# Entry of a recurrent attention layer: four layer norms and the masks at its head, V of the last tokens through seven SBUF tiles

## The chip, the cores and the metric

One core of a Trainium2 chip runs the whole program. The metric is the time of one execution on the device in microseconds (us), as the median of several runs.

The engines are PE (matmul, with PEld for its weight loads), DVE, ACT and POOL (elementwise work), and SP, which here only issues DMAs. Each engine works through its own queue in order.

## The reference

Four layers in a row, A B A B, each `x = x + layer(layernorm(x))` on x of 2048 tokens by 640, bf16 in and out.

- Layer A is causal attention of 32 heads of 20 in four segments of 512 tokens, with a compressive memory. Only its end matters here: an output projection by `a_wo` for each 128 tokens, the residual sum, and its stores.
- Layer B is a recurrent attention with 32 heads of 128. The tokens come in 64 segments of 32. Each step puts 8 memory rows ahead of its 32 tokens:

```
h = concat([mem, xs])                     # 8 + 32 rows
q, k, v = h@Wq, h@Wk, h@Wv                # 32 heads of 128
p = softmax(where(mask, q k^T * scale, -1e9))
o = (p v) @ Wo
mem = o[:8];  outs.append(o[8:])
```

So step s+1 needs the memory rows that step s has made: 64 steps in series, twice.

## The kernel before, in words

The functions `layer_A` and `layer_B` are called in turn. The arithmetic of layer B stands in one function: pools and constant tiles, then the **entry**, then a loop over 64 steps.

**A step** takes one block of 32 columns (8 memory rows and the first 24 tokens of a segment, in `HX`) through K, Q and V projections ("thin" matmuls, `thin_mm`, lines `b_Ka`, `b_Qa`, `b_Kb`, `b_Qb`, `b_Va`, `b_Vb`), transposes, scores, softmax, P V and the output projection `b_OPS`. The last 8 tokens of each segment ("tails", in `TX`) don't depend on the memory's recurrence in their projections, so they are done for eight segments at once: `tail_unit` makes K or Q of 8 heads for 64 rows, `vtail_unit` makes V of 512 columns for them. Their results go to DRAM (`QKd`, `VTd`, written by `tail_evac` and `vtail_evac`) and come back by segment (`tails_load`, `vtails_in`). There are 8 such units of each kind for a group of eight segments; a step does one of each for the group after.

**The entry** prepares the first group and the first segment:

1. Load four tiles of 128 tokens (`ln_load`, into the tiles xt, XO, XOd and tl of the pool bx), and `b_wv` in five chunks.
2. Layer norm of tiles 0 and 1 (`ln_norm`: DVE statistics, POOL power, DVE normalization), each followed by `ln_spread`: five PE transposes (`b_lntps`) and two ACT copies into `HX` and `TX`.
3. Eight tails (k = 0 to 7). ACT copies the even ones, DVE the odd ones, into `b_tu` tiles that take turns in the four buffers of the pool `kqp`; each copy is followed by a store to `QKd`. The norms of tiles 2 and 3 are put after tails 1 and 5, their spreads after tails 3 and 7.
4. K and Q projections of segment 0's block (`b_Kp`, `b_Qp`), copied by ACT (K) and DVE (Q) into four `b_kq` tiles, which share the four buffers of `kqp` with the tails. The eight chunks of `b_wo` (640 KB each) are loaded behind this in program order. Then transposes (`b_TP`) and copies into KT and QT.
5. `init_state`: two small sums for `b_sel`, zeros for XO, Px, Pm, QZ and HXz, and the additive masks: DVE fills `b_negs` and `b_maskf`, POOL runs 16 selects on `b_maskf`, DVE casts it to `b_mask12`. The tile `b_negs` lies in the buffer of PTa, `b_maskf` in that of OTsb, both in the pool `b_wk`, near the end of SBUF.
6. Eight V units (`vtail_unit(0, k)`), copied by DVE (even) and ACT (odd) into three tiles in turn (vt, E0, msb), each with two stores of 64 rows to `VTd`. Then two V projections (`b_V`), `vtails_in(0)`, and the first tail and V unit of the next group.

**What sets the order.** Inside layer B, `_OrdNC` (lines 89 to 119) chains the instructions of PE, ACT, DVE and POOL to program order, each engine for itself. SP isn't chained. Layer A chains only PE that way. A scheduler that runs when the program is built merges the queues of layer A's end with layer B's entry, with earlier program text first among what is ready. So the entry's first instructions stand in the same queues as layer A's last ones (`a_YP`, `a_xnew`, `a_xnb`).

The pools of a layer are laid over SBUF in the order in which they are opened, behind the constants and `b_wq`, `b_wk`; layer A's pools are closed before layer B's are opened, so both use the same bytes. A tile of layer B waits for the last reader of what lay there. PSUM tiles of layer B's entry (`ps_tile`) share five buffers.

All calls that record an instruction on an engine in this order show as line L101 in the profile (the helper's line), so instructions are named by their tiles. DMAs carry their own lines: L759 `ln_load`, L849 `tail_evac`, L869 `vtail_evac`, L822 `vtails_in`, L660 `b_wo`, L811 `tails_load`, L337 and L340 layer A's stores of x.

Of the kernel before, what the change touches and what calls it, by code (L numbers as in the profile page):

```python
# [18 lines left out]
F32 = mybir.dt.float32  # L19
BF16 = mybir.dt.bfloat16  # L20
# [648 lines left out]
def layer_B(nc, tc, C, W, x_src, xb_src, x_dst, mem0, B_Wv, B_Wo, nsteps=64, out_bf16=False, tag=""):  # L669
    SCB = 1.0 / math.sqrt(128.0)  # L670
    nc_raw = nc
    nc = _OrdNC(tc, nc_raw, engines=ORDER_ENGINES)
# [3 lines left out]
    VTd = tc.dram_tile([nsteps, 8, 4096], BF16, name=f"b_VTd{tag}")  # L676
    with ExitStack() as ctx:
# [6 lines left out]
        bx = pool("b_x", 1)  # L684
        sml = pool("b_sml", 2)
        kqp = pool("b_kqp", 4)
# [3 lines left out]
        wk = pool("b_wk", 1)  # L690
# [12 lines left out]
        Px = st.tile([128, 12, 32], BF16, name="b_Px")  # L703
        Pm = st.tile([128, 12, 32], BF16, name="b_Pm")
        mask12 = st.tile([128, 12, 40], BF16, name="b_mask12")
        QZ = [st.tile([128, 16, 24], BF16, name=f"b_QZ{i}") for i in range(2)]
# [1 line left out]
        HXz = st.tile([128, NCH, 1, 32], BF16, name="b_HXz")  # L708
        OTdef = [wk.tile([128, 32, 32], BF16, name=f"b_OTdef{i}") for i in range(2)]

        def init_state():
            nc.vector.tensor_tensor(out=selm[:, 0, :], in0=C.identb[:, 24:32], in1=C.identb[:, 88:96], op=ALU.add)
            nc.vector.tensor_tensor(out=selm[:, 1, :], in0=C.identb[:, 56:64], in1=C.identb[:, 120:128], op=ALU.add)
            XO_ = bx.tile([64, 320], F32, name="b_XO", tag="XO")
            nc.vector.memset(XO_[:], 0.0)
            XOd_ = bx.tile([64, 320], F32, name="b_XOd", tag="XOd")
            nc.gpsimd.memset(Px[:], 0.0)
            nc.gpsimd.memset(Pm[:], 0.0)
            for i in range(2):
                nc.gpsimd.memset(QZ[i][:], 0.0)  # L720
            negs = wk.tile([128, 32], F32, name="b_negs", tag="PTa")
            nc.vector.memset(negs[:], -1e9)
            maskf = wk.tile([128, 2, 40], F32, name="b_maskf", tag="OTsb")
            nc.vector.memset(maskf[:], 0.0)

            def above(out, rows, ncol, base, chan, colstep=1):
                nc.gpsimd.affine_select(out=out, in_=negs[rows, 0:ncol], pattern=[[colstep, ncol]], compare_op=ALU.is_gt,
                                        fill=0.0, base=base, channel_multiplier=chan)

            for i in range(4):  # L730
                r8, r16, r32 = (slice(32 * i, 32 * i + w_) for w_ in (8, 16, 32))
                above(maskf[r16, 0, 0:8], r16, 8, 8, -1)
                above(maskf[r8, 0, 0:8], r8, 8, 0, -1)
                above(maskf[r32, 1, 8:32], r32, 24, 0, -1)
                above(maskf[r32, 1, 0:8], r32, 8, 24, -1, 0)
            nc.vector.tensor_copy(mask12[:, 0:4, :], maskf[:, 0, :].unsqueeze(1).to_broadcast([128, 4, 40]))
            nc.vector.tensor_copy(mask12[:, 4:12, :], maskf[:, 1, :].unsqueeze(1).to_broadcast([128, 8, 40]))
            nc.gpsimd.memset(HXz[:], 0.0)
            return XO_, XOd_

        HX, TX, QT, KT, VH = {}, {}, {}, {}, {}
        ln_xt, ln_ready = {}, []
# [19 lines left out]
        def ln_norm(g):  # L762
            xt = ln_xt[g]
            layernorm_tile(nc, sml, C, xt[:], xt[:], "b_ln")
            ln_ready.append(g)

        def ln_spread(g):
            xt = ln_xt.pop(g)
            tps = ps_tile([128, NCH, 4, 32], BF16, "b_lntps")
            for c in range(NCH):  # L770
                nc.tensor.transpose(tps[:, c, :, :].rearrange("p i t -> p (i t)"), xt[:, 128 * c:128 * c + 128], C.identb[:])
            HX[g] = hp.tile([128, NCH, 4, 32], BF16, name="b_HX", tag="HX")
            T, half = divmod(g, 2)
            if half == 0:
                TX[T] = tx.tile([128, NCH, 8, 8], BF16, name="b_TX", tag="TX")
            nc.scalar.copy(HX[g][:, :, :, 8:32], tps[:, :, :, 0:24])
            nc.scalar.copy(TX[T][:, :, 4 * half:4 * half + 4, :], tps[:, :, :, 24:32])
# [73 lines left out]
        def vtail_unit(T, k, c0=0, c1=NCH, ps=None):  # L851
            b4, ch = divmod(k, 2)
            if ps is None:
                ps = ps_tile([128, 256], F32, "b_vtail")
            for c in range(c0, c1):
                for q in range(4):
                    n = 2 * b4 + q // 2
                    nc.tensor.matmul(ps[32 * q:32 * q + 32, :], lhsT=TX[T][:, c, 4 * (q % 2):4 * (q % 2) + 4, :].rearrange("p s t -> p (s t)"),
                                     rhs=W.wv[:, c, 512 * n + 256 * ch:512 * n + 256 * ch + 256],
                                     start=(c == 0), stop=(c == NCH - 1), tile_position=(0, 32 * q), skip_group_check=True)  # L860
            return ps

        def vtail_evac(T, k, ps, eng, home="vt"):
            b4, ch = divmod(k, 2)
            vt = wk.tile([128, 256], BF16, name="b_vt", tag=home)
            evac(eng, vt[:], ps[:])
            for jj in range(2):
                o = 512 * (2 * b4 + jj) + 256 * ch
                nc.sync.dma_start(VTd[8 * T:8 * T + 8, :, o:o + 256].rearrange("s t f -> (s t) f"), vt[64 * jj:64 * jj + 64, :])  # L869

        def wo_half(h, jj2):
            return W.wo[:, h, :].rearrange("p (c j x) -> p j c x", j=2, x=64)[:, jj2]
# [14 lines left out]
        n0 = min(4, NG)  # L887
        for g in range(n0):
            ln_load(g, homes[g])
        load_B_wv(nc, W, B_Wv)  # L890
        for g in range(min(2, n0)):
            ln_norm(g)
            ln_spread(ln_ready.pop(0))
        nc.gpsimd.memset(HX[0][:, :, 0, 0:8], 0.0)
        with nc.allow_non_contiguous_dma(reason="mem0 transpose load (tiny)"):
            for c in range(NCH):
# [1 line left out]
        for k in range(8):  # L898
            tail_unit(0, k, 0, 8, shared=True)
            tail_evac(0, k, "act" if k % 2 == 0 else "dve", (kqp, "kq"))  # L900
            if k % 4 == 1 and 2 + k // 4 < n0:
                ln_norm(2 + k // 4)
            if k % 4 == 3 and 2 + k // 4 < n0:
                ln_spread(ln_ready.pop(0))
        cols = cols_of(0)
        jobs = [(nm, b) for b in range(2) for nm in ("K", "Q")]
# [1 line left out]
        for nm, b in jobs:  # L908
            ps = thin_mm(cols, W.wk if nm == "K" else W.wq, b, f"b_{nm}p")
# [9 lines left out]
        XO, XOd = init_state()  # L919
        tails_copy(0, tails_load(0))  # L920
        Vth = VH[-1] = w2.tile([128, 2, 512], BF16, name="b_Vth", tag="Vth")
        for k in range(8):
            vtail_evac(0, k, vtail_unit(0, k), "dve" if k % 2 == 0 else "act", ("vt", "E0", "msb")[k % 3])
        for b in range(2):
            ps = thin_mm(cols, W.wv, b, "b_V")
            evac("act" if b == 0 else "dve", Vth[:, b, :], ps[:])
# [5 lines left out]

        def x_out(ops_, XO_, store, nm):
            nc.vector.tensor_tensor(out=XO_[:], in0=ops_[0:64, :], in1=XO_[:], op=ALU.add)
            if out_bf16:
                xo = wk.tile([64, 320], BF16, name=f"b_xnb{nm}", tag=f"xnb{nm}")
            else:
                xo = XO_
            nc.vector.tensor_tensor(out=xo[:], in0=ops_[64:128, :], in1=XO_[:], op=ALU.add)
            store(xo)  # L940
# [43 lines left out]
        for s in range(nsteps):  # L984
# [183 lines left out]
            if not last:  # L1168
                dst = cols_of(u + 1)
                msb = wk.tile([128, 320], BF16, name="b_msb", tag="msb")  # L1170
# [3 lines left out]
                for pi, (ca, cb) in enumerate(parts):  # L1174
                    mt = ps_tile([128, cb - ca, 8], F32, f"b_MT{pi}")
                    for c in range(ca, cb):
                        for q in range(4):
                            o = 64 * c + 32 * (q % 2)
# [119 lines left out]
```

## Time and profile before

| what | value |
|---|---|
| median of 3 runs | 2735.45 us (2733.53 to 2737.24) |
| the profiled execution | 2729.23 us |
| its span, first to last instruction | 2727.5 us |
| PE busy | 2570.4 us (94%) |
| DVE, ACT, POOL busy | 1688.7, 1580.8, 719.3 us |
| mean granted PE clock | 0.988 of full speed |
| entry of the first layer B: first b_lntps to the first step's b_Ka | 355.33 to 405.82 us |
| the same of the second layer B | 1714.26 to 1761.82 us |
| first step: b_Ka to the next b_Ka | 14.52 us in each |
| PE busy in 355.30 to 390.30, and its granted clock | 28.88 us, 0.79 |
| PE busy in 390.30 to 405.82, and its granted clock | 11.07 us, 0.78 |
| PE busy in 405.82 to 420.34, and its granted clock | 14.27 us, 1.00 |

How to read it: times in the timeline are counted from the span's start. A line of the timeline gives start, duration, engine, operation, tile written and tiles read, shapes and count; in square brackets stands the idle time of that engine before it, and what ended the wait. Where several matmuls are merged into a line, the duration goes to the end of the last, which overlaps the next line's start; the time from start to start is the one to add. The granted clock is the share of PE's full clock that the chip allowed.

### The profile page before, as it was taken

How to read it: one execution, taken by the hardware profiler on the slowest of the kernel's cores; microseconds unless marked ns; L12 is line 12 of the kernel's file. 1: busy time of each engine (PE TensorE's matmuls, PEld its weight loads, DVE VectorE, ACT ScalarE, POOL GpSimd, SP SyncE). 2: the span in 40 equal slices, each digit the busy share in tenths (PEclk: the TensorE clock that was granted, in tenths of full speed). 3: DMA queues.
4: the chain of work that ended last, by engine and by line, in shares of the span. 5: the costliest groups of instructions: out<-in, count | busy, mean ns of one | idle time of the engine just before them, and what ended most of it. 6: DMA issues, size and time to landing. Idle time of an engine off the chain costs nothing. (4 is left out here: it accounts for less than half of the span.)

```text
span 2727.5 us, 146862 instructions
## 1 busy us (share of the span) xinstructions
PE 2570.4 (94%) x65416; PEld 1691.3 (62%) x65480; DVE 1688.7 (62%) x4553; ACT 1580.8 (58%) x3708; POOL 719.3 (26%) x1645
## 2 busy tenths in 40 slices
PE   5999979999999999999989999799999999999998
PEld 3565556666666666666655565566666666666665
DVE  6999935555555555555589998355555555555554
ACT  4998935555555555554459889355555555555543
POOL 4677631111111111111146776211111111111110
PEclk9999979999999999999989999899999999999999
DMA  6111262221212121211130113611111111121110
GB/s 244 38 48 43 70 200 43 46 44 42 45 42 46 43 46 42 43 39 32 25 118 16 64 51 110 180 42 41 40 41 42 42 41 43 38 43 40 38 26 19
DMA packets 322298, 156.34 MB, mean 57 GB/s; under 512 B 245760, under 2 KB 310400, under 8 KB 318592
## 3 DMA queue, kind: packets, MB, share of 16 engines
q1 hardware_dynamic: 320224, 136.47, 19.7%
q8 instruction: 512, 8.39, 1.3%
q10 hardware_dynamic: 1440, 10.49, 1.1%
q14 instruction: 122, 1.00, 0.1%
HBM read 95.15 MB, written 51.71 MB: 54 GB/s over the span
## 5 line engine op out<-in xcount | busy, mean ns | idle before, releaser
L101 PEld LDWEIGHTS <-b_HX 128*32 128x32 bf16 x15360 | 425.5, 97 | 347.3 <-issue 16.2
L101 POOL TENSOR_TENSOR b_Pm<-b_E,b_rs 128x96 bf16<-128x96 bf16 x128 | 63.3, 494 | 1442.4 <-ACT b_Vth L101 1102.8
L130 DVE TENSOR_REDUCE a_nm<-a_S 128x2 f32<-128x512 f32 (+3 forms) x512 | 394.9, 815 | 44.7 <-PE a_S L101 36.9
L130 ACT ACTIVATE a_PT<-a_T 128x1024 bf16<-128x1024 f32 (+1 forms) x384 | 345.0, 902 | 25.9 <-PE a_T L101 17.8
L101 PE MATMUL b_OPS<-b_wo,b_OTsb 128*32 128x320 bf16 x8192 | 309.9, 302 | 11.1 <-issue 8.7
L101 PEld LDWEIGHTS <-b_OTsb 128*32 128x32 bf16 x8192 | 201.6, 97 | 97.8 <-DVE b_OTsb L101 24.5
L101 DVE CAST b_HX<-b_MT 128x8 bf16<-128x8 f32 x372 | 63.5, 172 | 279.1 <-PE b_MT L101 273.9
L130 POOL TENSOR_SCALAR_AFFINE_SELECT a_PT<-a_PT 128x256 bf16<-128x256 bf16 (+1 forms) x384 | 191.1, 509 | 134.8 <-ACT a_PT L130 133.1
L101 ACT CAST b_msb<-b_OPS 128x64 bf16<-128x64 f32 x378 | 69.4, 256 | 237.3 <-PE b_OPS L101 237.3
L101 ACT CAST b_kq<-b_Kb 128x512 bf16<-128x512 f32 x128 | 74.9, 585 | 201.9 <-PE b_Kb L101 201.9
L101 DVE COPY b_KT<-b_TPak 128x128 bf16<-128x128 bf16 x128 | 28.7, 224 | 227.5 <-PE b_TPak L101 227.5
L101 PE MATMUL b_Va<-b_wv,b_HX 128*32 128x512 bf16 x2520 | 160.6, 380 | 0.0
L101 DVE TENSOR_SCALAR b_kq<-b_Qa 128x512 bf16<-128x512 f32 x128 | 88.5, 691 | 116.1 <-PE b_Qa L101 113.3
L101 PE MATMUL b_Vb<-b_wv,b_HX 128*32 128x512 bf16 x2520 | 159.9, 379 | 0.0
L101 PEld LDWEIGHTS <-b_kq 128*128 128x128 bf16 x2080 | 116.8, 98 | 68.8 <-ACT b_kq L101 55.6
L101 PE MATMUL b_Ka<-b_wk,b_HX 128*32 128x512 bf16 x2520 | 159.1, 379 | 0.1
L101 PE MATMUL b_Qa<-b_wq,b_HX 128*32 128x512 bf16 x2520 | 158.8, 379 | 0.0
L101 PE MATMUL b_Kb<-b_wk,b_HX 128*32 128x512 bf16 x2520 | 158.8, 379 | 0.0
L101 PE MATMUL b_Qb<-b_wq,b_HX 128*32 128x512 bf16 x2520 | 158.7, 379 | 0.0
L101 DVE CAST b_OTsb<-b_OTP 128x160 bf16<-128x160 f32 (+1 forms) x384 | 122.2, 373 | 39.9 <-PE b_OTP L101 39.9
L101 PE MATMUL b_vtail<-b_wv,b_TX 128*32 128x256 bf16 x2880 | 136.9, 271 | 7.8 <-issue 4.7
L101 PE MATMUL a_T<-a_q,a_kT 32*128 32x512 bf16 (+3 forms) x1024 | 121.6, 299 | 23.5 <-DVE a_nm L130 16.1
(194 smaller groups left out, 5723.7 us busy)
## 6 DMA issues: line engine op xcount, KB each, us to landing
b_QKd<-b_tu SPq DMA_DIRECT2D x128, 128.0 KB
b_tl<-b_QKd SPq DMA_DIRECT2D x128, 128.0 KB
b_wv<-in_B_Wv_dram SPq DMA_DIRECT2D x10, 1024.0 KB
b_wo<-in_B_Wo_dram SPq DMA_DIRECT2D x16, 640.0 KB
b_VTd<-b_vt SPq DMA_DIRECT2D x256, 32.0 KB
b_Vth<-b_VTd SPq DMA_DIRECT2D x512, 16.0 KB
b_XO<-xres SPq DMA_DIRECT2D x256, 30.0 KB
b_wk<-in_B_Wk_dram ACTq DMA_DIRECT2D x5, 1024.0 KB
```

Source lines behind the costliest of these rows:

```text
L101: r = f(*a, **k)
L130: r = f(*a, **k)
```

## The change

Four edits, all in `layer_B`.

- `init_state` is split. The masks and `b_sel` become `init_masks`; the zeros stay in `init_state`.
- All four norms run ahead of the tails, in the same loop; only tiles 0 and 1 are spread there. `init_masks` follows, still ahead of the zeroing of HX and of the tails. The spreads of tiles 2 and 3 come after tails 1 and 3 instead of 3 and 7.
- The eight V copies go to seven tiles: vt, E0, msb, the four buffers of `kqp`, and vt again for the eighth.
- The two stores of a V unit become one store of 128 rows. This holds in the steps as well.

```diff
-        def init_state():
+        def init_masks():
             nc.vector.tensor_tensor(out=selm[:, 0, :], ...)
             nc.vector.tensor_tensor(out=selm[:, 1, :], ...)
...
             nc.vector.tensor_copy(mask12[:, 4:12, :], ...)
+
+        def init_state():
+            XO_ = bx.tile([64, 320], F32, name="b_XO", tag="XO")
+            nc.vector.memset(XO_[:], 0.0)
+            XOd_ = bx.tile([64, 320], F32, name="b_XOd", tag="XOd")
+            nc.gpsimd.memset(Px[:], 0.0)
+            nc.gpsimd.memset(Pm[:], 0.0)
+            for i in range(2):
+                nc.gpsimd.memset(QZ[i][:], 0.0)
             nc.gpsimd.memset(HXz[:], 0.0)
             return XO_, XOd_
...
-        def vtail_evac(T, k, ps, eng, home="vt"):
+        def vtail_evac(T, k, ps, eng, home=None):
             b4, ch = divmod(k, 2)
-            vt = wk.tile([128, 256], BF16, name="b_vt", tag=home)
+            pool_, tg = home or (wk, "vt")
+            vt = pool_.tile([128, 256], BF16, name="b_vt", tag=tg)
             evac(eng, vt[:], ps[:])
-            for jj in range(2):
-                o = 512 * (2 * b4 + jj) + 256 * ch
-                nc.sync.dma_start(VTd[8 * T:8 * T + 8, :, o:o + 256].rearrange("s t f -> (s t) f"), vt[64 * jj:64 * jj + 64, :])
+            dr = VTd[8 * T:8 * T + 8, :, 1024 * b4:1024 * b4 + 1024].rearrange("s t (j c f) -> c j (s t) f", j=2, f=256)[ch]
+            nc.sync.dma_start(dr, vt[:])
...
-        for g in range(min(2, n0)):
+        for g in range(n0):
             ln_norm(g)
-            ln_spread(ln_ready.pop(0))
+            if g < 2:
+                ln_spread(ln_ready.pop(0))
+        init_masks()
         nc.gpsimd.memset(HX[0][:, :, 0, 0:8], 0.0)
...
             tail_evac(0, k, "act" if k % 2 == 0 else "dve", (kqp, "kq"))
-            if k % 4 == 1 and 2 + k // 4 < n0:
-                ln_norm(2 + k // 4)
-            if k % 4 == 3 and 2 + k // 4 < n0:
+            if k in (1, 3) and ln_ready:
                 ln_spread(ln_ready.pop(0))
...
+        vt_homes = [(wk, "vt"), (wk, "E0"), (wk, "msb")] + [(kqp, "kq")] * 4 + [(wk, "vt")]
         for k in range(8):
-            vtail_evac(0, k, vtail_unit(0, k), "dve" if k % 2 == 0 else "act", ("vt", "E0", "msb")[k % 3])
+            vtail_evac(0, k, vtail_unit(0, k), "dve" if k % 2 == 0 else "act", vt_homes[k])
```

More of the change, by code (lines that the diff above doesn't have):

```diff
@@ L709, in layer_B @@
         OTdef = [wk.tile([128, 32, 32], BF16, name=f"b_OTdef{i}") for i in range(2)]
-        def init_state():
+        def init_masks():
             nc.vector.tensor_tensor(out=selm[:, 0, :], in0=C.identb[:, 24:32], in1=C.identb[:, 88:96], op=ALU.add)
             nc.vector.tensor_tensor(out=selm[:, 1, :], in0=C.identb[:, 56:64], in1=C.identb[:, 120:128], op=ALU.add)
[L714 to L720, printed above, removed]
             negs = wk.tile([128, 32], F32, name="b_negs", tag="PTa")
```

## The prediction, made before the change was run

> **What bounds the kernel.** The page's first part, busy time by engine, gives PE 2570.4 of 2727.5 us (94%); in the chain of waits nearly every step is a PE group of layer B, each following the one before. One step of layer B takes 14.5 us (Ka starts at 405.82 and again at 420.34), of which PE is busy 14.27 by the windows. So a microsecond taken from PE's path ahead of the first step of a layer B moves the end by a microsecond, once for each of the two layers B. The change touches that entry, and one store in each step. I read PE's timeline there, then for each of its gaps the engine that ended it. Entry one on PE:
>
> ```profile
> 372.85 4.83 PE L101 MATMUL b_tail<-b_TX,b_wk 128*128 128x64 bf16 x160
> 381.68 0.71 PE L101 MATMUL b_lntps<-c_identb,b_xt 128*128 128x128 bf16 x5 [4.00 <-DVE b_xt L101]
> 382.32 2.32 PE L101 MATMUL b_Kp<-b_wk,b_HX 128*32 128x512 bf16 x20
> 384.43 2.35 PE L101 MATMUL b_Qp<-b_wq,b_HX 128*32 128x512 bf16 x20
> ...
> 389.10 1.27 PE L101 MATMUL b_TP<-c_identb,b_kq 128*128 128x128 bf16 x16
> 390.30 3.46 PE L101 MATMUL b_vtail<-b_wv,b_TX 128*32 128x256 bf16 x120
> 395.16 1.28 PE L101 MATMUL b_vtail<-b_wv,b_TX 128*32 128x256 bf16 x40 [1.40 <-DVE b_vt L101]
> 399.48 4.46 PE L101 MATMUL b_V<-b_wv,b_HX 128*32 128x512 bf16 x40 [3.04 <-ACT b_vt L101]
> 403.87 1.47 PE L101 MATMUL b_tail<-b_TX,b_wq 128*128 128x64 bf16 x40
> ```
>
> Three gaps: 4.00 us before the transposes of the fourth normalized tile, 1.40 and 3.04 for copies of the V tails. After the long ones the matmuls take twice as long: Kp 2.11 us from start to start, against 1.08 in a step. The engines behind the gaps:
>
> ```profile
> 376.66 0.89 DVE L130 TENSOR_TENSOR a_xnew<-a_YP,a_xr 128x320 f32<-128x320 f32 x2 [3.20 <-DMA xres<-a_xnew]
> 377.47 0.68 DVE L101 CAST b_tu<-b_tail 128x512 bf16<-128x512 f32 x1
> 378.06 0.88 DVE L101 BATCH_NORM_STATS2 b_ln_st<-b_xt 128x6 f32<-128x320 bf16 x2
> ...
> 380.04 1.58 DVE L101 TENSOR_SCALAR b_xt<-b_xt,b_ln_mv,b_ln_rstd 128x640 bf16<-128x640 bf16 x1 [0.66 <-POOL b_ln_rstd L101]
> ...
> 394.00 0.78 DVE L101 CAST b_mask<-b_maskf 128x160 bf16<-128x160 f32 x2 [2.96 <-POOL b_maskf L101]
> ```
> ```profile
> 391.19 3.12 POOL L101 TENSOR_SCALAR_AFFINE_SELECT b_maskf<-b_negs 16x8 f32<-16x8 f32 x16 [9.75 <-DVE b_maskf L101]
> ```
> ```profile
> 399.06 0.37 ACT L101 CAST b_vt<-b_vtail 128x256 bf16<-128x256 f32 x1 [7.06 <-DMA b_VTd<-b_vt]
> ```
>
> DVE normalizes the fourth tile only after the copy of tail 5, which had stood behind layer A's last sum. Later it waits for POOL's masks with the first V copy queued behind. Then ACT waits 7.06 us for the store that frees the first V tile.
>
> **Block V** (transposes to the first step). In the profile it lasts 390.30 to 405.82, 15.52 us; in entry two 1746.69 to 1761.82, 15.13. The masks leave DVE's queue here, which frees the first V copy; seven tiles (the four b_kq among them, whose transposes are then done) let seven copies run without waiting for a store; the eighth waits for the first store. PE's own work: a V unit at full clock is 0.545 us (2.18 us for four, the group of six less the group of two), eight are 4.36; two V projections 2.16 at a step's 1.08; the next tail 1.40 (start to start), its V unit 0.55. Sum 8.5, so 7.0 and 6.6 us can go. What is late next is DMA: the wo chunks fill the queue until about 396.5 (365 GB/s to 396, then 145), and stores stand behind them. The eighth copy and ACT's copies after it can land there, though later projections need few of them. I set 1.5 us aside in each entry for this and for a lower clock: **5.5 and 5.1 us**.
>
> **Block T** (the tails to the transposes). Norms three and four go ahead of the tails. DVE was free from 358.17 but for three short sums, and all four loads were issued by 349.3, so they are ready about 363. Their work of 2.3 us each (0.88 + 0.21 + 0.15 + 0.66 wait + 0.45) may push a sum of layer A back; 0.5 us per entry for that. The 4.00 us gap goes (3.91 in entry two), and Kp to Qp shrinks from 6.78 (382.32 to 389.10) to 4.32, in entry two from 5.51. At most 6.4 and 5.1 us.
>
> But the masks now stand in DVE's queue between the norms and the copy of tail 1, and they are not free there. By the tile sizes, with the pools of both layers laid over the same bytes in the order opened, b_negs and b_maskf lie inside layer A's a_wo, so their memsets wait for layer A's last matmul with it: 371.69, in entry two 1727.40. Then 0.2 of memsets, 3.12 of selects, 0.78 of casts: DVE is free at 375.8 (1731.5), where tail 1 was copied at 368.37 (1724.16). Behind it are tails 1, 3, 5 and 7. PE goes on as long as ACT's tails free PSUM tiles; one of five tiles may make it wait about 1.5 us. The longer path runs through the four b_kq tiles: copy of tail 1, its store, copy of tail 5 into that tile, its store, copy of the first Q projection. A copy is 0.69. A store takes 2.6 us (tail 3: issued 379.4, tail 7's copy released 382.0) to 6.3 (tail 2: 371.80 to 378.07); I take 2.6, since the slow one shared the queue with two wo chunks and a 320 KB store. Then 375.8 + 0.8 + 2.6 + 0.7 + 0.3 + 2.6 gives 382.8, with 0.7 for tail 3's copy between 383.5, where the Q copy ran at 386.83: 3.3 us earlier. Entry two: 1739.2 against 1743.45, 4.2. Less the 0.5: **2.8 and 3.7 us**.
>
> At full length: the HX memset and the memsets of Px, Pm and QZ also queue behind the masks on POOL; their readers (Kp at 378, the first step) come later. They may run beside the casts; beside them the normalization took 1.58 us, against 0.45 alone, so the casts could cost 1.1 more per entry; kept in the range. The Trainium skill, SBUF — State Buffer, "SBUF: two separate sides", gives this as a rule that speaks against the move: such a VectorE operation and a GpSimd one exclude each other for a whole instruction. By it the sum would be 2.2 us smaller, and the row agrees.
>
> **Stores in the steps.** SP issues one store instead of two, each 0.58; both lie beside a PE-bound step, as SP has idle time in it, and the V tile was waited for by nothing that PE needed. Cost 0; up to 0.1 us per step either way if the one store, with twice the rows, lands later than the pair: no row shows it, and the next use of the tile is 14 us on.
>
> **Sum.** 5.5 + 2.8 in entry one, 5.1 + 3.7 in entry two: 17.1 us. The profiled execution took 2729.23 us, 1.7 more than its span, so it would take 2712.1. The median of the timed runs is 2735.45, 6.2 above it; the gaps are the same in each, so **2718.4**.
>
> The lower clock: after 4.00 us of idling PE's granted clock was 0.50 from 382 to 386, after 3.04 it was 0.50 from 398 to 404, after 1.40 it stayed 1.00. The Trainium skill, TensorE: Matmul & The Clock Gate, Part 1, puts the idle window at about 3.4 us. By that page a 3.04 us wait need not be punished and my 1.5 us per entry would be partly too much, a sum nearer 18.5; the trace says it can be.
>
> **Rivals.**
> 1. *All of it goes*: stores land before they are asked for. 7.0 + 6.4 + 6.6 + 5.1 = 25.1 us, 2710.3. For it: DVE idle before and after the tails. Against: the wait on a_wo and the wo chunks. 0.12.
> 2. *Half*: block T's gain is given back by PSUM tiles held by four DVE tails, or block V's by stores behind wo. 5.5 to 11 us, 2724 to 2730, say 2727. 0.13.
> 3. *Nothing to see*: the stalls are replaced. Two stores of 6.3 us in series put the first Q copy at 390.9, 4.1 late, and the PE gap before it halves the clock for the V block, some 2.3 us (4.46 against 2.16 for the V projections); 7.0 - 4.1 - 2.3 leaves 0.6 each, 2734. For it: tail 2's 6.3. 0.14.
> 4. *Slower*: the stores of tails 1 and 5, in series, stand behind wo chunks. The Q copy comes at 378.3 + 2L, L being issue to landing; against 386.83, with 4.7 left of block V, it turns at L = 6.6 us. At the longest landing here (b_tl issued 388.56, used 398.08: 9.5) the Q copy is 10.5 late, 5.8 lost per entry, 2747. For it: SP issues wo chunks whenever nothing else is ready. Against: only two chunks had been issued by 378. 0.09.
> 5. *It does not do what it says*: V copies wait anyhow, because the store count was not what held them. The rows say they waited for tiles, and the tiles change; it is within case 2.
>
> **Numbers.** Forecast (gain 11 to 21 us, 2714 to 2724) 0.52, cases 1 to 4 as above. A measurement here tells about 0.2%, 5.5 us, from no change. Faster by more 0.77, within 0.14, slower 0.09. To leave out no more than 2 in 10 the range runs from case 1's 2710 to 2732, inside case 3.
>
> **What would show it.** Right: no gap on PE before the fourth b_lntps, its mean granted clock 1.00 through Kp and Qp, V projections of 2.2 us for both, DVE's V copies with no POOL wait before them, ACT's 7.06 us wait gone or at the eighth copy only. b_maskf's selects at about 372 and 1728, right behind layer A's last a_YP, and DVE's copy of tail 1 after them, near 376. Wrong: selects before 365 (no wait on a_wo; then nearer case 1), a new PE gap at tails 4 to 6 (PSUM) or before the b_TP transposes (b_kq stores), or a step longer than 14.5 us.

## The result, and the profile after

| what | before | after |
|---|---|---|
| median of 11 runs each, one chip | 2733.53 us (2726.75 to 2737.24) | 2739.9 us (2736.94 to 2743.42) |
| ratio, 95% interval | | 1.0025 (1.0016 to 1.0034) |
| span of the profiled execution | 2727.5 us | 2735.7 us |
| entry one: first tail to first V unit, V block, first step | 26.33, 15.52, 14.52 | 26.61, 11.09, 21.36 |
| entry two: the same | 26.56, 15.13, 14.52 | 27.26, 10.68, 21.52 |

The kernel became slower by 0.25%, 6.4 us, where a gain of 17.1 us was forecast. The V block did shrink, by 4.4 us in each entry. Then the first step of each layer B, which the forecast left at 14.5, took 21.4 us.

PE's timeline of after, entry one. Columns as before: start, duration, what it does, and in brackets the idle time before it with what ended it.

```profile
377.04 1.26 PE L101 MATMUL b_Kp<-b_wk,b_HX 128*32 128x512 bf16 x20
378.13 1.25 PE L101 MATMUL b_Qp<-b_wq,b_HX 128*32 128x512 bf16 x20
...
386.28 0.40 PE L101 MATMUL b_TP<-c_identb,b_kq 128*128 128x128 bf16 x4 [1.87 <-ACT b_kq L101]
388.82 0.61 PE L101 MATMUL b_TP<-c_identb,b_kq 128*128 128x128 bf16 x4 [2.14 <-DVE b_kq L101]
389.35 7.18 PE L101 MATMUL b_vtail<-b_wv,b_TX 128*32 128x256 bf16 x160
396.36 2.33 PE L101 MATMUL b_V<-b_wv,b_HX 128*32 128x512 bf16 x40
...
400.45 1.25 PE L101 MATMUL b_Ka<-b_wk,b_HX 128*32 128x512 bf16 x20
...
409.26 0.59 PE L101 MATMUL b_TPak<-c_identb,b_kq 128*128 128x128 bf16 x4 [4.33 <-DVE b_vt L101]
...
412.28 2.34 PE L101 MATMUL b_Va<-b_wv,b_HX 128*32 128x512 bf16 x20
```

All three gaps of before are gone: the fourth `b_lntps` waits for nothing, and the eight V units run as one line. But the transposes `b_TP` now come one by one with gaps of 1.87 and 2.14, and a new gap of 4.33 us stands inside the first step. After it the matmuls run at half clock: `b_Va` takes 2.10 from start to start, where 1.08 is usual. The 6.84 us that the step grew are the gap and this.

DVE's timeline of after:

```profile
370.15 0.09 DVE L101 MEMSET b_negs<- 128x32 f32 x1 [1.25 <-PE a_YP L101]
...
373.30 0.67 DVE L101 CAST b_mask<-b_maskf 128x160 bf16<-128x160 f32 x2 [2.98 <-POOL b_maskf L101]
373.89 0.67 DVE L101 TENSOR_SCALAR b_tu<-b_tail 128x512 bf16<-128x512 f32 x1
...
379.07 0.69 DVE L101 CAST b_tu<-b_tail 128x512 bf16<-128x512 f32 x1 [3.12 <-DMA b_QKd<-b_tu]
381.85 0.69 DVE L101 CAST b_tu<-b_tail 128x512 bf16<-128x512 f32 x1 [2.08 <-DMA b_QKd<-b_tu]
383.26 0.69 DVE L101 TENSOR_SCALAR b_kq<-b_Qp 128x512 bf16<-128x512 f32 x1 [0.72 <-DMA b_QKd<-b_tu]
388.07 0.69 DVE L101 TENSOR_SCALAR b_kq<-b_Qp 128x512 bf16<-128x512 f32 x1 [4.11 <-DMA b_QKd<-b_tu]
...
408.79 0.42 DVE L101 CAST b_vt<-b_vtail 128x256 bf16<-128x256 f32 x1 [9.28 <-DMA b_VTd<-b_vt]
409.13 0.68 DVE L101 TENSOR_SCALAR b_kq<-b_Qa 128x512 bf16<-128x512 f32 x1
```

The line at 408.79 is the copy of the **next group's** first V unit. Its tile is "vt", which the eighth V of this group has; so it waits 9.28 us for the eighth's store. The copy of `b_Qa` is queued behind it, and PE needs both. ACT meets the same stores, since the first step's `b_kq` tiles are the four buffers that the fourth to seventh V sit in. ACT's timeline of after:

```profile
398.11 0.37 ACT L101 CAST b_vt<-b_vtail 128x256 bf16<-128x256 f32 x1 [2.19 <-DMA b_VTd<-b_vt]
...
402.65 0.59 ACT L101 CAST b_kq<-b_Ka 128x512 bf16<-128x512 f32 x1 [2.06 <-DMA b_VTd<-b_vt]
405.66 0.59 ACT L101 CAST b_kq<-b_Kb 128x512 bf16<-128x512 f32 x1 [2.42 <-DMA b_VTd<-b_vt]
```

SP's timeline of after, the eight stores of the entry and one in a step:

```profile
391.12 12.91 SPq L871 DMA_DIRECT2D b_VTd<-b_vt  x8
...
410.48 0.52 SPq L871 DMA_DIRECT2D b_VTd<-b_vt  x1
```

One store by itself takes SP 0.52 us to issue. From the first of the eight to the end of the last it is 12.91, and that is not the stores' time alone. The third holds SP for 3.40 us, until 396.65: up to about 396 the chunks of `b_wo`, issued just ahead, keep all DMA engines busy (share 1.06 in 394 to 396). The last five, with `b_wo` out of the way, still start 1.4 to 1.5 us apart. PE's windows show what the wait costs (stretch, length, PE busy, granted clock, DMA share, GB/s):

```profile
402.00:406.00 4.00, 2.94 (x56) 1.00 0.14 43
406.00:410.00 4.00, 0.72 (x6) 0.80 0.25 74
410.00:412.00 2.00, 2.00 (x54) 0.50 0.51 93
```

With stores queued up, the DMA engines are 0.14 busy, some 2.2 of 16. That alone doesn't tell how many engines a store uses: e1 (below), whose queued stores run on 16, has 0.18 in 402 to 406. The packets do. The page's line on DMA, of before, of after and of experiment e3 (below):

```profile
DMA packets 322298, 156.34 MB, mean 57 GB/s; under 512 B 245760, under 2 KB 310400, under 8 KB 318592
```
```profile
DMA packets 318458, 156.32 MB, mean 57 GB/s; under 512 B 241921, under 2 KB 306561, under 8 KB 314753
```
```profile
DMA packets 320249, 156.32 MB, mean 58 GB/s; under 512 B 243712, under 2 KB 308352, under 8 KB 316544
```

In the trace's packet records every DMA engine that takes part in a store ends it with a packet of 4 bytes. Two stores per unit are 256 in the program, one is 128. Had each still run on 16 engines, there would be 128 x 16 = 2048 packets fewer. There are 3840 fewer, which is 256 x 16 - 128 x 2: the one store runs on **two** engines. Its pattern in DRAM is two halves of 64 rows, an outer dimension of two. The Trainium skill, DMA: Bandwidth & Descriptors, "Rules for kernel authors", says that an outermost dimension smaller than 16 confines a DMA to at most that many engines. The packets agree: 2 here, and in e3, whose 128 rows lie at one stride, 322298 - 320249 = 2049, so 16. (Of the packets of 4 bytes alone, before has 22401, after 18561 and e3 20353: 3840 and 2048 fewer.)

The rest of the 8.2 us between the spans: entries +2.69 and +3.25 from the first tail on, the first tail 1.23 earlier and 1.96 later, the further steps up to the start of the last -1.6 and +2.9, the end +0.3.

### The profile page after: what moved, and what is told of

Read it like the earlier page. It is cut to its first block, busy times and chain, and to the rows that moved or that the text cites. A ratio compares the mean times of both kernels' runs of the same rounds, so it can differ in the third digit from the quotient of the medians.

```text
span 2735.7 us, 146707 instructions
## 1 busy us (share of the span) xinstructions
PE 2576.1 (94%) x65480; PEld 1694.4 (62%) x65480; DVE 1684.4 (62%) x4553; ACT 1585.4 (58%) x3708; POOL 721.2 (26%) x1645
## 4 chain that ended last, share of the span: by engine, by line
PE 78%; DVE 11%; ACT 6%; DMA 3%; issue 2%; POOL 1%; SPq 0%; ACTq 0%; DVEq 0%; POOLq 0%
PE b_OPS L101 10%; PE b_tail L101 5%; DVE a_nm L130 5%; PE b_Ka L101 5%; PE b_Qb L101 5%; PE b_Qa L101 5%; PE b_Kb L101 5%; PE b_Va L101 5%; PE b_Vb L101 4%; PE b_SP L101 4%; PE b_OTP L101 3%; PE b_vtail L101 3%; PE b_OPSd L101 3%; PE b_PTP L101 3%; ACT a_PT L130 3%; PE a_S L101 2%
## 5 line engine op out<-in xcount | busy, mean ns | idle before, releaser
L130 ACT ACTIVATE a_PT<-a_T 128x1024 bf16<-128x1024 f32 (+1 forms) x384 | 345.6, 904 | 25.9 <-PE a_T L101 17.9
L101 ACT ACTIVATE b_E<-b_SP 128x320 bf16<-128x320 f32 (+1 forms) x256 | 81.2, 369 | 110.4 <-PE b_Va L101 93.9
```

The lines of the kernel that those rows point to most:

```text
L101: r = f(*a, **k)
L130: r = f(*a, **k)
```

## The experiments

Theory **narrow store**: the one store of after is slow, and that moves the wait into the first step. Rival **shared tile**: the tiles alone do it, with any store. For the transposes, theory **store chain** against the forecast. Each group of kernels ran with the kernel before on one chip; the chips differ (the kernel before had medians of 2713.2, 2724.9, 2714.0 and 2719.2 us), so ratios are compared. "Entry" gives first tail to first V unit (T), V block (V) and first step (S), for entry one / two. They come from one profiled execution of each kernel: in the five kernels that leave the tails as they were, T alone scatters from 23.9 to 26.3 in entry one.

| kernel | T | V | S | ratio to before, 95% interval |
|---|---|---|---|---|
| before | 26.3 / 26.6 | 15.5 / 15.1 | 14.5 / 14.5 | 1 |
| after | 26.6 / 27.3 | 11.1 / 10.7 | 21.4 / 21.5 | 1.0025 (1.0016 to 1.0034) |
| e1 after, two stores | 26.3 / 26.9 | 10.5 / 11.2 | 17.5 / 17.6 | 0.9998 (0.9988 to 1.0008) |
| e2 before, one store | 23.9 / 25.5 | 16.1 / 15.5 | 14.5 / 14.5 | 1.0009 (1.0000 to 1.0019) |
| e3 after, rows in line | 25.5 / 26.5 | 10.6 / 10.3 | 14.5 / 14.5 | 0.9981 (0.9972 to 0.9990) |
| e4 after, eighth V apart | 26.5 / 27.1 | 10.4 / 10.1 | 17.9 / 18.3 | 1.0016 (1.0005 to 1.0028) |
| e5 e3 without the move | 25.1 / 26.0 | 10.9 / 10.2 | 14.6 / 14.8 | 0.9956 (0.9941 to 0.9971) |
| e6 before, the move | 25.8 / 25.9 | 14.5 / 15.6 | 14.5 / 14.6 | 1.0007 (0.9997 to 1.0017) |
| e7 e3, tails apart | 19.9 / 20.7 | 15.9 / 17.9 | 16.7 / 16.4 | 0.9985 (0.9974 to 0.9997) |
| e8 e7, masks split | 19.9 / 19.7 | 16.9 / 15.5 | 16.2 / 16.3 | 0.9982 (0.9973 to 0.9991) |
| e9 e8, V apart | 19.4 / 20.6 | 12.0 / 8.5 | 15.9 / 19.7 | 0.9958 (0.9943 to 0.9973) |
| e10 e9, b_wo later | 20.7 / 21.1 | 9.7 / 8.8 | 16.3 / 15.9 | 0.9936 (0.9922 to 0.9951) |
| e11 before, seven tiles | 24.5 / 25.8 | 10.2 / 10.1 | 20.9 / 19.6 | 1.0000 (0.9989 to 1.0011) |
| e12 before, rows in line | 25.0 / 25.3 | 12.7 / 15.4 | 14.5 / 14.5 | 0.9996 (0.9985 to 1.0007) |
| e13 e3, masks back | 25.3 / 25.3 | 10.6 / 10.1 | 14.8 / 14.6 | 0.9973 (0.9964 to 0.9983) |
| e14 e10, masks back | 20.4 / 20.0 | 10.2 / 10.2 | 15.8 / 15.7 | 0.9943 (0.9929 to 0.9956) |

### e1: two stores again

```diff
-            nc.sync.dma_start(dr, vt[:])
+            for jj in range(2):
+                o = 512 * (2 * b4 + jj) + 256 * ch
+                nc.sync.dma_start(VTd[8 * T:8 * T + 8, :, o:o + 256].rearrange("s t f -> (s t) f"), vt[64 * jj:64 * jj + 64, :])
```

> The kernel after, with the two stores of 64 rows put back; all else as after. Theory 'narrow store': the store of 128 rows moves its data through only a few DMA engines, 1.45 us apart each, so the eighth lands 8 us after its copy, and the next group's first V copy, which takes the same tile, holds DVE for 9.28 and 10.70 us. With two stores the lane takes some 1.2 us per unit and each lands 2 us after its issue: the first step falls from 21.4 and 21.5 us to 14.5 to 15.5, some 6.5 us less per entry, and the time is about 2727 where the kernel after has 2740: faster than the kernel before by 0.2 to 0.3%. Rival 'shared tile': the wait comes from the eighth V and the next one sharing a tile, and V tiles sitting in the buffers of K and Q, with any store: the first step stays above 19 us and the time within 2 us of the kernel after.

The first step fell to 17.5, not to 14.5, and the ratio is 0.9998, not 0.9975. Both theories miss. DVE's, SP's and PE's timelines of e1:

```profile
406.87 0.42 DVE L101 CAST b_vt<-b_vtail 128x256 bf16<-128x256 f32 x1 [8.22 <-DMA b_Vth<-b_VTd]
```
```profile
391.54 13.78 SPq L872 DMA_DIRECT2D b_VTd<-b_vt  x16
```
```profile
407.95 0.40 PE L101 MATMUL b_TPaq<-c_identb,b_kq 128*128 128x128 bf16 x4 [2.85 <-DVE b_kq L101]
```

From the first to the last, sixteen stores on 16 engines occupy SP as long, 13.78 us, as eight on two, 12.91. In both, part of that is `b_wo`: here SP issues three stores between 394.41 and 399.13, and 2.9 us of its waits end with a chunk of `b_wo` that lands. The last ten, in a row, take 6.2 us, so 1.24 per unit where the narrow store takes 1.4 to 1.5. The DVE copy waits 8.22 us in place of 9.28. (Its releaser is put down to the read-back `b_Vth`, which follows the last store.) The gap on PE is 2.85 in place of 4.33 and stays at full clock, so the step loses 3 us and not 7. What counts is when the **last** of the V stores lands, and both forms of the store are late. How much of that is `b_wo` and how much the queue itself isn't separated here: no run moves `b_wo` in the kernel after.

### e2: the merged store alone

```diff
 (before)
-            for jj in range(2): ...
+            dr = ...
+            nc.sync.dma_start(dr, vt[:])
```

> The kernel before, with only the one store of 128 rows per V unit. 'Narrow store': eight stores need some 12 us of the lane, a copy waits for the store three units earlier, and the next group's first V copy waits for the store of the seventh unit: V block and first step together 3 to 7 us longer per entry (before: 15.52 + 14.52 and 15.13 + 14.52), total 2739 to 2747. 'Shared tile': the eighth V has a tile of its own turn here, so one store in place of two costs nothing: 2733.5 within 2.

V block and first step 30.6 and 30.0 us, against 30.04 and 29.65: 0.6 and 0.3 more, well under the 3 to 7 forecast. With three tiles in turn the stores are spread over the V block (SP issues them in three groups, of three, three and two), and SP never has eight queued. The narrow store alone costs at most 0.19%.

### e3: one store, its 128 rows at one stride

```diff
-    VTd = tc.dram_tile([nsteps, 8, 4096], ...)
+    VTd = tc.dram_tile([NT, 4, 128, 512], ...)
...                                     (vtails_in reads it in that order)
-            nc.sync.dma_start(dr, vt[:])
+            nc.sync.dma_start(VTd[T, b4, :, 256 * ch:256 * ch + 256], vt[:])
```

> The kernel after, still with one store of 128 rows, but the DRAM tensor laid out so that the 128 rows follow each other at one stride, where after has two halves of 64 rows as an outer dimension; the reading back moves the same rows of 1 KB. 'Narrow store', in its form that the outer dimension of two is what is shared out among the DMA engines: 16 completion packets per store again where after makes 2, the store lands 2 to 2.5 us after its issue, the first step falls to 14.5 to 15.5 us, total 2725 to 2728. If it is the 128 rows in one DMA and not their pattern, or if 'shared tile' holds: no change from after within 2.

As the theory says: 16 engines (the packets above), the first step 14.50 in both entries. SP's timeline of e3, then DVE's:

```profile
389.18 7.38 SPq L870 DMA_DIRECT2D b_VTd<-b_vt  x8
```
```profile
398.33 0.42 DVE L101 CAST b_vt<-b_vtail 128x256 bf16<-128x256 f32 x1 [1.65 <-PE b_vtail L101]
400.44 0.69 DVE L101 TENSOR_SCALAR b_kq<-b_Qa 128x512 bf16<-128x512 f32 x1 [1.68 <-DMA b_Vth<-b_VTd]
```

Eight stores now take SP 7.38 us, much of which it waits for copies and for `b_wo`: a store by itself takes 0.32 us. The copy into the shared tile waits for PE, no longer for a store. The tiles are those of after, and `b_wo` stands where it stood: a shared tile costs nothing once the stores are out in time. The ratio, 0.9981, is at the upper edge of what I expected (0.9969 to 0.9980).

### e4: the eighth V in a tile of its own

```diff
-        vt_homes = [...] + [(kqp, "kq")] * 4 + [(wk, "vt")]
+        vt_homes = [...] + [(kqp, "kq")] * 4 + [(wk, "OTsb")]
```

> The kernel after, with the eighth V in a tile that nothing else needs until late in the first step, so that the next group's V copy doesn't wait for its store. 'Narrow store': the copies of K and Q still wait for the stores of the fourth to seventh V (402.65 to 407.18 in after), so the first step falls only from 21.4 to some 18 to 20 us, 1.5 to 3.5 us less per entry, total 2733 to 2737. 'Shared tile': the first step falls to about 15 us, total 2727.

17.9 and 18.3, at the lower edge of the narrow store's bounds. The time came out less well: 1.0016, where I expected up to 1.0013. ACT's timeline of e4:

```profile
403.75 0.59 ACT L101 CAST b_kq<-b_Ka 128x512 bf16<-128x512 f32 x1 [3.20 <-DMA b_VTd<-b_vt]
406.77 0.59 ACT L101 CAST b_kq<-b_Kb 128x512 bf16<-128x512 f32 x1 [2.43 <-DMA b_VTd<-b_vt]
408.29 0.60 ACT L101 ACTIVATE b_kq<-b_Qb 128x512 bf16<-128x512 f32 x1 [0.94 <-DMA b_VTd<-b_vt]
```

Half of the step's growth is the shared "vt", the other half the four `b_kq` buffers, lent to V tiles whose stores are still queued.

### e11 and e12: the tiles alone, the better store alone

```diff
 e11 (before, two stores)
-            vtail_evac(0, k, ..., ("vt", "E0", "msb")[k % 3])
+            vtail_evac(0, k, ..., vt_homes[k])
 e12 (before, three tiles): e3's two edits
```

> The kernel before, with the seven tiles for V alone: two stores of 64 rows, norms and masks as before. From e1 (which has the move too): 16 stores take SP some 13 us, the eighth V copy waits for the first store and the next group's V copy, in the same tile, for the eighth's: V block 10.5 to 12 us, first step 16.5 to 18 us, 1.5 to 3 us less per entry than before (30.04 and 29.65 us), ratio 0.9980 to 0.9995. Prediction's rival on the homes: V block some 10 us and first step 14.5, ratio 0.9960 to 0.9970.

> The kernel before, with only the store merged to 128 rows at one stride (DRAM laid out for it); three tiles for V by turns, norms and masks as before. e2, with the store of after, took 16.03 and 15.39 us for the V block and 14.52 for the first step. 'Narrow store': 16 completion packets per store; the turns of three tiles still wait for a store's landing each, some 2 us after its issue whether it is one or two: V block 13.5 to 15.5, first step 14.5, ratio 0.9985 to 1.0. If merging were worth much by itself: V block under 12 us, ratio below 0.998.

e11: the V block is 10.2 and 10.1, and the first step 20.9 and 19.6. All of the gain is given back, as in after, with the old stores. That is the rival **shared tile**, as far as two stores go; the step is even longer than the 16.5 to 18 that I took from e1, since the gap on PE is longer and half clock follows it (0.50 in 410 to 414, where e1 has 1.00), and the ratio misses the 0.9980 to 0.9995 that I expected. DVE's, SP's and PE's timelines of e11:

```profile
408.10 0.42 DVE L101 CAST b_vt<-b_vtail 128x256 bf16<-128x256 f32 x1 [8.87 <-DMA b_Vth<-b_VTd]
```
```profile
395.04 11.52 SPq L870 DMA_DIRECT2D b_VTd<-b_vt  x16
```
```profile
409.19 0.61 PE L101 MATMUL b_TPaq<-c_identb,b_kq 128*128 128x128 bf16 x4 [3.91 <-DVE b_kq L101]
```

e12: no change that can be told (entry one's V block, 12.7, is below the 13.5 to 15.5 expected). So the tiles alone are worth 0, the store in line alone 0, and both together (e5, next) 0.44%. Tiles let the copies run ahead, and only a short store queue lets that last.

### e5, e6, e13: the move of norms and masks

```diff
 e5: e3 without the move        e6: before with the move alone
 e13: e3, and
-        init_masks()            (at the head)
+        init_masks()            (ahead of the V units)
```

> The kernel of e3 (store of 128 rows at one stride, seven tiles for V), with the norms of tiles 2 and 3 and the masks back where they are in the kernel before. e3 took 10.57 and 10.26 us for the V block, 14.50 for the first step, and from the first tail to the end of the transposes b_TP 25.6 and 26.5 us (before: 26.40 and 26.63). Theory 'store chain': what ends the transposes' stretch is the turn of four buffers between tails, their stores and the K and Q copies, so the place of norms and masks is worth nothing there: 24 to 27 us again; but the masks stand before the V copies on DVE once more, and the V block takes 13 to 15 us. Total 0 to 0.15% under the kernel before, 1 to 5 us above e3's ratio of 0.9981. Rival, the prediction's: the move is worth 2.8 and 3.7 us in the stretch of the transposes: that stretch 28.5 and 30 us, total at or above the kernel before.

> The kernel before, with only the norms and the masks moved to the head as in the kernel after; V in three tiles by turns and two stores of 64 rows as before. 'Store chain': K's projection starts some 4 us earlier, and the wait for the tails' stores takes its place, so tails and transposes still take 25.5 to 27.5 us; the V block loses only the masks on DVE, 1 to 2 us of 15.5, since its copies then wait for the stores three units before. Total within 3 us of the kernel before (ratio 0.999 to 1.001). Prediction's: 2.8 and 3.7 us less in the transposes' stretch, and V's block shorter: ratio 0.996 to 0.9975.

> The kernel of e3 with only the masks back ahead of the V units; the norms of tiles 2 and 3 stay at the head. From the first tail to the end of the transposes the kernels with the move took 25.6 to 27.3 us, those without it 24.0 to 26.6. Theory 'masks hold the tails': DVE stands at layer A's last use of the bytes and at POOL in front of the second tail's copy, so the stores of tails 1, 3, 5, 7 start some 4 us later, and the K and Q copies take their buffers in turn; without that the gain that was forecast for the norms comes: that stretch 22 to 24 us, the V block 10 to 11.5, first step 14.5 to 14.8, ratio to the kernel before 0.9930 to 0.9955. Rival 'stores of the last tails behind b_wo': tails 4 to 7 wait for the stores of tails 0 to 3 whatever the masks do: 25 to 27 us, ratio 0.9955 to 0.9980.

The move is worth nothing in the transposes' stretch. T over all kernels with four shared buffers for the tails: without the move (before, e2, e5, e11, e12) 25.0 / 25.8 us on average, with all of it (after, e1, e3, e4, e6) 26.1 / 26.7, with the norms alone (e13) 25.3 / 25.3. So the move costs some 1 us rather than gaining any. That this is the masks and not the norms rests on the one profile of e13 and is no more than likely. e6, the move alone, agrees: 25.8 and 25.9, ratio 1.0007; its V block became shorter by 1.0 in entry one and longer by 0.5 in entry two, where 1 to 2 less were expected. In e13 the masks were gone from the tails, and something else took their place. DVE's timeline of e13, then ACT's:

```profile
377.67 0.89 DVE L130 TENSOR_TENSOR a_xnew<-a_YP,a_xr 128x320 f32<-128x320 f32 x2 [4.80 <-DMA xres<-a_xnew]
378.48 0.68 DVE L101 TENSOR_SCALAR b_tu<-b_tail 128x512 bf16<-128x512 f32 x1
...
384.86 0.69 DVE L101 CAST b_tu<-b_tail 128x512 bf16<-128x512 f32 x1 [5.11 <-DMA b_QKd<-b_tu]
```
```profile
385.63 0.59 ACT L101 CAST b_kq<-b_Kp 128x512 bf16<-128x512 f32 x1 [5.42 <-DMA b_QKd<-b_tu]
```

Layer A's last sum holds the second odd tail, and then the stores hold the last tails and K. The theory "masks hold the tails" falls; the rival that I wrote beside it stands.

My numbers for e5 failed: a V block of 10.9 and 10.2, where 13 to 15 were expected from the masks on DVE, and a time 0.44% under the kernel before, where at most 0.15% was expected. DVE's timeline of e5, then PE's:

```profile
393.97 0.96 DVE L101 CAST b_mask<-b_maskf 128x160 bf16<-128x160 f32 x2 [2.97 <-POOL b_maskf L101]
```
```profile
390.79 6.95 PE L101 MATMUL b_vtail<-b_wv,b_TX 128*32 128x256 bf16 x160
```

DVE's first V copy came 4.4 us after the units began, and PE ran through all eight: five PSUM tiles and ACT's copies cover it. e5, e3 and e13 have entries of the same length (from the first tail 101.6, 101.9 and 100.7 us for both together), yet ratios of 0.9956, 0.9981 and 0.9973, each from another group and chip. Where the 0.25% between e5 and e3 lies isn't settled.

### e7 and e8: tails in eight tiles

```diff
 e7 (from e3)
-            tail_evac(0, k, ..., (kqp, "kq"))
+            tail_evac(0, k, ..., ([(kqp, "kq")] * 4 + [(wk, "tu"), (w2, "QT"), (w2, "Vth"), (w2, "Vth")])[k])
 e8 (from e7): fills and selects behind tail 1, casts in init_state
```

> The kernel of e3, with the fifth to eighth tail in four other tiles, so that neither a tail's copy nor a copy of K or Q waits for a store of a tail issued a moment before. 'Store chain': from K's first projection to the end of the transposes 6.5 to 7.5 us where e3 has 11.3 and 11.5, and the gaps of DVE and ACT that end with a store of b_QKd (2 to 6 us each) are gone; tails and transposes together 4 to 6 us shorter per entry, of which the V block may give back up to 2 where b_wo is still landing. Total 6 to 10 us under e3, ratio to the kernel before about 0.9950. Rival: something else is due at the same time (b_wo's chunks on the DMA engines, the masks on DVE before the second tail): less than 1.5 us per entry, ratio 0.9970 to 0.9985.

> The kernel of e7, with the masks' fills and POOL's selects behind the second tail's copy, and DVE's two casts of them only ahead of the V units, so that DVE stands for neither layer A's last use of the bytes (1.25 us) nor POOL (2.98 us) in front of the second tail's copy. 'Masks hold the tails': the second tail's copy comes some 4 us earlier, the tails' stretch falls by 1 to 3 us per entry, total 2 to 5 us under e7. 'Covered': PE had four more PSUM tiles to fill, and nothing changes within 1 us.

The store chain is shown: from Kp to the first V unit 5.63 and 5.77 us (e3: 11.21 and 11.46; 6.5 to 7.5 expected), and T 5.6 and 5.8 shorter. But the V block grew by 5.3 and 7.6. ACT's, SP's and PE's timelines of e7:

```profile
398.17 0.37 ACT L101 CAST b_vt<-b_vtail 128x256 bf16<-128x256 f32 x1 [11.55 <-DMA b_VTd<-b_vt]
```
```profile
384.61 4.55 SPq L660 DMA_DIRECT2D b_wo<-in_B_Wo_dram  x5
389.34 1.23 SPq L813 DMA_DIRECT2D b_tl<-b_QKd  x1
390.61 8.28 SPq L870 DMA_DIRECT2D b_VTd<-b_vt  x8
```
```profile
398.60 2.33 PE L101 MATMUL b_Ka<-b_wk,b_HX 128*32 128x512 bf16 x20 [7.27 <-ACT b_vt L101]
```

V came 5 us earlier, but its stores stand behind five chunks of `b_wo`, which keep all DMA engines busy until 397. The eighth V waits for the first store, in the tile that they share. So the rival of e7 came true: `b_wo` was due at the same time, and the ratio is 0.9985. Where the masks stand (e8) makes no difference: "covered".

### e9, e10, e14: V in tiles of its own, b_wo behind the V stores

```diff
 e9 (from e8)
-        vt_homes = ...
+        vt_homes = [(wk, "PTb"), (wk, "E0"), (wk, "msb"), (bx, "xt"), (kqp, "kq"), (wk, "OTsb"), (kqp, "kq"), (wk, "PTa")]
 e10 (from e9): load_B_wo(k) for k = 3 to 7 behind the V units
 e14 (from e10): init_masks() ahead of the V units
```

> The kernel of e8, with no two of the eight V copies in a tile that something needs soon (PTb, E0, msb, xt, OTsb, PTa, and two buffers of K and Q). In e7 the eighth V copy waited 11.55 us on ACT for the first V store, since that store stood behind five chunks of b_wo until 397. Theory 'b_wo in front': without the shared tile the V block falls to 8.5 to 10 us (e7: 15.85 and 17.82), but two copies of the first step still wait for V stores that land behind b_wo, and b_Vth comes late, so the first step takes 15.5 to 19 us; entries 2 to 6 us shorter than in e8 each, ratio to the kernel before 0.9935 to 0.9970. Rival: b_wo itself ends last, for b_OPS, and nothing is gained over e8's 0.9982 within 0.0008.

> The kernel of e9, with five of the eight chunks of b_wo written behind the eight V stores instead of ahead of the transposes. 'b_wo in front': V stores land some 2 us after their copies, no copy of the first step waits for them, the first step's K to V part has no gap, but its output projection then waits for the last chunk of b_wo: the five chunks need some 12 us of all DMA engines; together 0 to 3 us less per entry than e9. Rival, 'b_wo ends last': b_OPS waits 2 to 6 us for b_wo and the entry is longer than e9's.

> The kernel of e10 (tails and V copies in tiles of their own, store at one stride, five chunks of b_wo behind the V stores) with the masks wholly ahead of the V units, as in the kernel before. In e5 the masks' 4 us on DVE there cost nothing (V block 10.80 and 10.14), since PE had five PSUM tiles to fill. 'Covered': V block within 1 us of e10's 9.66 and 8.75, ratio within 0.0015 of e10's 0.9936. Rival: with V copies no longer waiting for stores, the first V copy's 4 us wait shows: V block 2 to 4 us longer, ratio 0.9950 to 0.9965.

e9's ratio is within its bounds, 0.9958; the V block of entry one (12.0) and the first step of entry two (19.7) are beyond theirs. e10 gains 0.7 and 2.9 us per entry on it, as "b_wo in front" has it, but not that no copy would wait. In ACT's timeline of e10 K of the second half still waits for a V store in its buffer:

```profile
402.38 0.58 ACT L101 CAST b_kq<-b_Kb 128x512 bf16<-128x512 f32 x1 [3.98 <-DMA b_VTd<-b_vt]
```

e10 is the fastest, **0.9936** (0.9922 to 0.9951): some 17 us under the kernel before. That is what the change was forecast to give, but here five further edits give it: the store at one stride, tails and V in tiles of their own, the masks split, and `b_wo` later. Output projections didn't wait for `b_wo`. e14 is level with it; its V block in entry two, 10.2 against 8.8, is 0.4 beyond the 1 us that I allowed.

## Why the prediction was wrong

**The step that failed** is in block V: "The eighth copy and ACT's copies after it can land there, though later projections need few of them", with 1.5 us set aside. The sum stopped at the first step's `b_Ka` and took that step as it was. But the fourth to seventh V sit in the very buffers of the first step's K and Q, and the eighth in that of the next group's V. Each V tile that doesn't wait any more hands its wait to the tile's next user. I looked at who held PE up before, and not at who takes the tiles next. It cost 6.84 and 7.0 us, against the 4.43 and 4.45 that block V gained. e11 shows that the seven tiles do this with the old stores too; e3 and e5 show that they don't when the eight stores are out in 7.38 and 4.35 us. Even before, the copy of the next group's first V unit waited for a store, as a line of DVE's timeline of before shows:

```profile
408.04 0.42 DVE L101 CAST b_vt<-b_vtail 128x256 bf16<-128x256 f32 x1 [3.36 <-DMA b_VTd<-b_vt]
```

The copy of `b_Qa` behind it ended at 409.06, and PE asked for it at 410.48: that wait was hidden by some 1.4 us, and the change brought PE here earlier while the last store came no earlier.

Over the profiled executions the result lies 25.3 us above the forecast (8.2 more in place of 17.1 less): 13.8 in the first steps, 7.5 in block T, 1.7 in block V, 2.3 elsewhere. The 1.5 us set aside per entry in block V for stores and clock were about the right size for block V itself (1.1 and 0.7 short).

**Stores in the steps: cost 0.** For the steps nothing speaks against it: e2 and e12 are within 0.19% of before, and over all profiles the steps behind the first scatter by some 10 us per layer with no order by the store. In the entry it was wrong. I wrote that no row shows the one store. By the rule of the Trainium skill that is named above (DMA: Bandwidth & Descriptors, "Rules for kernel authors"), it would run on two engines at most. In after each takes 1.4 to 1.5 us in a row, where a pair had taken 1.4 (six stores in 4.12 us from 395.13 of before). So halving the number of stores saved no time, and the last one landed only at 408.8.

**Block T.** The waits named were right: the selects came right behind layer A's last `a_YP` (370.46 and 1730.44; forecast about 372 and 1728), the copy of the second tail at 373.89 (about 376), the first Q copy at 383.26 (383.5). The gap before the fourth `b_lntps` went. But the sum ended at the first Q copy. The second takes the buffer of tail 7, whose store stood behind a chunk of `b_wo`, and came at 388.07. Tail 7 was copied at 381.85 in after, at 382.00 in before: the move brought PE to Kp about 4 us earlier and left the end of the chain where it was. In before the wait for that store was hidden behind the gap that I took away: the second Q copy waited for PE. DVE's timeline of before:

```profile
382.00 0.69 DVE L101 CAST b_tu<-b_tail 128x512 bf16<-128x512 f32 x1 [0.38 <-DMA b_QKd<-b_tu]
...
389.22 0.69 DVE L101 TENSOR_SCALAR b_kq<-b_Qp 128x512 bf16<-128x512 f32 x1 [1.70 <-PE b_Qp L101]
```

Expected -2.8 and -3.7, measured +0.28 and +0.70. The 1.1 us that the masks' casts might have lost beside POOL's memsets didn't come: they took 0.67 us in both entries, 0.78 and 0.77 before.

**The clock.** The prediction took from before's 3.04 us wait that such a wait halves the clock. In finer windows of before the clock falls at about 397.35, only 0.9 us into that wait (396.44 to 399.48). Ahead of it stand the gap of 1.40 and 1.28 us of matmuls, so this row doesn't show what 3.04 us alone would do.

**Rivals.** The fourth was the nearest in kind: it had stores behind `b_wo` make it slower. Its place was wrong; it put the delay at tails 1 and 5, and it stands at tail 7 (mildly) and at the first V stores. `b_wo` isn't the whole cause: e3, with `b_wo` in the same place, has a first step of 14.5. The fifth, that V copies wait anyhow because the store count isn't what held them, was dismissed with "the tiles change": e11 shows that tiles without a shorter queue are worth nothing. It should have had a price of its own.

**Right:** that PE's entry sets the end, to within some 5 us of scatter (over both entries, e10 is 20.0 us shorter from the first tail on, and 0.64%, 17 us, faster; e3 is 10.6 shorter and 5 faster), that DVE's masks wait for layer A's bytes, and that three gaps would go.

## What to carry to other kernels

When copies get more tiles, list who takes each tile next, and when the store that frees it lands: the wait moves there, if the queue of stores is no shorter. Count the time of a queue and not its entries: merging two DMAs into one whose outermost dimension is two left the queue as long, and the same merge at one stride shortened it to 7.4 us and less. Two edits that are worth nothing alone can be worth 5 to 12 us together (e3 and e5), so undo and try them in pairs.

## What the runs showed of the hardware

- In these runs a store's outermost dimension sets how many DMA engines carry it: 2 completion packets per store with an outermost dimension of 2, and 16 with one of 64 or 128.
- Issuing is held up with it: 0.52 us for a lone narrow store, 1.39 to 1.41 for each in a row, 1.4 to 1.5 from start to start. In a row, two stores of 64 rows on 16 engines took 1.24 us per unit (e1). Eight stores of 128 rows at one stride took 4.93 and 4.35 us where copies were ready (e13, e5).
- The clock: a gap of 2.85 us on PE (e1) left it at full. In gaps of 4.00 (before), 3.91 (e11) and 4.33 (after) it fell to half 2.6 to 3.5 us after work had stopped, and stayed there for about 6.8 us each time. In before it fell 0.9 us into the gap of 3.04, with a gap of 1.40 and 1.28 us of matmuls ahead of it. In after two gaps of 1.87 and 2.14 with 0.40 us of matmuls between them did so as well (0.50 in 390 to 394). So a sum over short gaps counts, and not the longest alone.
